# Running only the expert blocks that hold tokens: 24 fixed blocks and an eight-way dispatch

## The chip, the cores and the metric

The kernel runs on one core of one Trainium2 chip. The metric is the device time in microseconds of one execution, and lower is better. Before the change the median of three runs is 627.48 us, the fastest 621.67 us and the slowest 633.91 us.

## The reference

A gated linear attention is followed by a mixture of eight experts. Attention has batch 4, 8 heads, 768 tokens and 48 columns a head:

```python
for t in range(S):
    state = alpha[:, :, t, :, None] * state + np.einsum('bhd,bhe->bhde', k[:, :, t], v[:, :, t])
    y[:, :, t] = np.einsum('bhd,bhde->bhe', q[:, :, t], state)
```

Its output, as 3072 tokens of 384 columns, is `x`. The cosine router gives each token the expert whose embedding is nearest to it, and a gate weight. Each expert then handles its own tokens alone, with `w1[e]` of 384 x 1024 and `w2[e]` of 1024 x 384:

```python
for e in range(E):
    mask = expert_idx == e
    if not mask.any():
        continue
    h = np.maximum(x[mask] @ w1[e], 0.0)
    out[mask] = gate_w[mask, None] * (h @ w2[e])
```

All values are 32-bit floats. How many tokens an expert gets depends on the inputs, which are made from a fixed seed.

## The kernel before

The work has three stages. The first is attention (L99 to L339): 24 chunks of 128 tokens, all heads of a chunk at a time, with the steps of four chunks overlapped. It leaves the rows of `x` in DRAM (`x_rows`) and each token's expert and gate on the chip.

The second is the routing (L342 to L423). Tokens are sorted by expert into blocks of 128 rows, and every expert begins a new block. `nb` is the number of blocks of each expert and `start` the block at which an expert begins. A product of one-hot matrices (`inv`, L398) turns the sort around into `gidx`, the token that each row of each block reads, and `sidx`, the token that it is written to. A row without a token reads token 0 and is written nowhere. `eblk` holds the expert of each block, and `fresh` says whether the block's weights differ from those in its buffer.

The third stage is the experts (L426 to L502). 3072 tokens fill at least 24 blocks, and eight experts with a part-filled last block each can make them 31 (`NBLK`). The kernel runs all 31 in one unrolled loop (L439), however many hold tokens. A block j has these steps, each on its own engine:

- SP reads two numbers into registers (L441, L447) and issues the loads of `w1` and `w2` (L451, L454), 1.5 MB each, into buffer j % 2. From block 2 on, the loads are conditional on `fresh`.
- POOL gathers 128 rows of `x_rows` into `xg` (L459).
- PE turns `xg` in three transposes into `pxg` (L469), and DVE copies it to `xgT` (L471).
- PE multiplies by `w1` into `ph` (L478, 48 matmul instructions), and ACT applies the relu into `hT` (L484).
- PE multiplies by `w2` into `pyo` (L488, 16 instructions), DVE scales by the gate into `y` (L492), and POOL scatters `y` to the output rows (L493).

The scheduler orders the instructions of each engine ahead of time, within straight code. Each engine runs its own list in order and waits by semaphores only. `xg` and `xgT` have three buffers each, so POOL gathers several blocks ahead of PE, and the transposes of two blocks usually stand together ahead of a `ph`. At the end (L528) every engine drains, and SP waits for the last scatters.

Of the kernel before, what the change touches and what calls it, by code (L numbers as in the profile page):

```python
# [9 lines left out]
FP32 = mybir.dt.float32  # L10
I32 = mybir.dt.int32
AF = mybir.ActivationFunctionType
ALU = mybir.AluOpType
# [10 lines left out]
def kernel(  # L24
# [12 lines left out]
    nc = tc.nc  # L37
# [1 line left out]
    E, DM = expert_emb.shape  # L39
    F = w1.shape[2]  # L40
    P = 128
    DP = 64  # a head's columns, padded so that two heads fill the partitions
    NP = H // 2  # pairs of heads
    NCH = S // P  # chunks of a sequence
    N = B * S
    NS = N // P  # slots: token = slot * P + partition
    KT = DM // P
    FT = F // P
    # every expert's tokens fill whole blocks of P rows but for its last one
    NBLK = (N + E * (P - 1)) // P  # L50
    FAR = 1 << 20  # a row index out of bounds: the row is skipped

    x_rows = nc.dram_tensor("x_rows", (N, DM), FP32, kind="Internal").ap()

    consts = ctx.enter_context(tc.tile_pool(name="consts", bufs=1))

# [1 line left out]
    ident = consts.tile([P, P], FP32)  # L58
    make_identity(nc, ident)
    causal = consts.tile([P, 1, P], FP32)  # [j, i] = 1 where j <= i  # L60
    make_upper_triangular(nc, causal[:, 0], val=1.0, diag=True)
    earlier = consts.tile([P, P], FP32)  # [j, i] = 1 where j < i
    make_upper_triangular(nc, earlier, val=1.0, diag=False)
    ones = consts.tile([P, P], FP32)
    nc.gpsimd.memset(ones, 1.0)
    zeros = consts.tile([P, P], FP32)
    nc.gpsimd.memset(zeros, 0.0)
    half = consts.tile([P, NP, 2], FP32)  # which head of the pair a partition is of
    nc.gpsimd.memset(half, 0.0)
    nc.gpsimd.memset(half[0:DP, :, 0:1], 1.0)  # L70
    nc.gpsimd.memset(half[DP:P, :, 1:2], 1.0)
# [3 lines left out]
    nc.vector.tensor_copy(cols, cols_i)  # L75
    toks_i = consts.tile([P, NS], I32)
    nc.gpsimd.iota(toks_i, pattern=[[P, NS]], base=1, channel_multiplier=1)
    toks = consts.tile([P, NS], FP32)  # token + 1
    nc.vector.tensor_copy(toks, toks_i)
    first = consts.tile([P, E], FP32)  # E, E-1, ..: the first of equal logits wins  # L80
    nc.vector.tensor_scalar(first, cols[:, 0:E], -1.0, float(E), ALU.mult, ALU.add)

# [1 line left out]
    lg = consts.tile([P, NS, E], FP32)  # L84
    sq = consts.tile([P, NS], FP32)
    gate = consts.tile([P, NS], FP32)
# [7 lines left out]
    bgate = consts.tile([P, NBLK], FP32)  # L94
    eblk = consts.tile([1, NBLK], I32)
    fresh = consts.tile([1, NBLK], I32)

    # ==== gated linear attention, a chunk of P tokens of all heads at a time ====
    with ExitStack() as c1:  # L99
        pads = c1.enter_context(tc.tile_pool(name="pads", bufs=1))  # L100
        loads = c1.enter_context(tc.tile_pool(name="loads", bufs=6))
# [84 lines left out]
            nc.sync.dma_start(out=vt, in_=v_r[b, c])  # L186

        def decays(s):
            """q and k, head columns on the partitions, with the decays of the chunk.

            a: products of alpha from the chunk's start; r: of those after a token.
            The decay from token j to token i is a[i] / a[end] * r[j].
            """
            c = s % NCH
            d = st[s]
            i = s % NBUF
            pa = turned(at_s[i], "pa")
            a = work.tile([P, NP, P], FP32, name="a")
            r = r_s[s % NR]
            for p in range(NP):  # L200
                nc.vector.tensor_tensor_scan(a[:, p], pa[:, p], zeros, 1.0, ALU.mult, ALU.add)  # L201
                nc.vector.tensor_tensor_scan(  # L202
                    r[:, p, P - 2 :: -1], pa[:, p, P - 1 : 0 : -1], zeros[:, 0 : P - 1],
                    1.0, ALU.mult, ALU.add,
                )
            end = a[:, :, P - 1 : P]
            rend = work.tile([P, NP, 1], FP32, name="rend")
            nc.vector.reciprocal(rend, end)
            if c > 0:
                d["ends"] = ends = work.tile([P, NP, 2], FP32, name="ends", bufs=3)  # L210
                nc.gpsimd.tensor_tensor(ends, half, end.to_broadcast([P, NP, 2]), ALU.mult)
            pk = turned(kt_s[i], "pk")
            d["kr"] = kr = work.tile([P, NP, P], FP32, name="kr", bufs=3)
            nc.vector.tensor_tensor(kr, pk, r, ALU.mult)  # L214
            pq = turned(qt_s[i], "pq")
            d["qs"] = qs = work.tile([P, NP, P], FP32, name="qs", bufs=4)
            for p in range(NP):
                nc.vector.scalar_tensor_tensor(  # L218
                    out=qs[:, p], in0=pq[:, p], scalar=rend[:, p], in1=a[:, p],
                    op0=ALU.mult, op1=ALU.mult,  # L220
                )

        def update(s):
            """The state at the chunk's end, and its decayed form that the queries meet."""
            c = s % NCH
            d = st[s]
            vt, kr = d["vt"], d["kr"]
            decayed = None
            if c > 0:
                d["decayed"] = decayed = work.tile([P, NP, 2, D], FP32, name="decayed", bufs=3)  # L230
                nc.gpsimd.tensor_tensor(  # L231
                    decayed, carried["state"], bc(d["ends"], [P, NP, 2, D], 3), ALU.mult
                )
            if c == NCH - 1:
                return
            pkb = ps_tr.tile([P, NP, P], FP32, tag="tr", name="pkb")
            for p in range(NP):
                nc.tensor.transpose(pkb[:, p], kr[:, p], ident)  # L238
            kb = work.tile([P, NP, P], FP32, name="kb")
            nc.scalar.copy(kb, pkb)  # L240
            pd = ps_mm.tile([P, 512], FP32, tag="mm", name="pd")
            for p in range(NP):
                nc.tensor.matmul(  # L243
                    pd[:, 2 * p * D : 2 * (p + 1) * D],
                    lhsT=kb[:, p],
                    rhs=vt[:, 2 * p : 2 * p + 2].rearrange("p h d -> p (h d)"),
                    start=True, stop=True,
                )
            carried["state"] = state = work.tile([P, NP, 2, D], FP32, name="state")
            sflat = state.rearrange("p n j e -> p (n j e)")  # L250
            if decayed is None:
                nc.scalar.copy(sflat, pd[:, 0:DM])
            else:
                nc.vector.tensor_tensor(  # L254
                    sflat, pd[:, 0:DM], decayed.rearrange("p n j e -> p (n j e)"), ALU.add
                )

        def scores(s):
            """scores[j, i] of every head, zero where j > i."""
            d = st[s]  # L260
            kr, qs = d["kr"], d["qs"]
            d["sm"] = sm = work.tile([P, 2, NP, P], FP32, name="sm")
            sc = ps_sc.tile([P, 2, NP, P], FP32, name="sc")
            for p in range(NP):
                for hh in range(2):
                    sl = slice(DP * hh, DP * hh + DP)
                    nc.tensor.matmul(  # L267
                        sc[:, hh, p], lhsT=kr[sl, p], rhs=qs[sl, p], start=True, stop=True
                    )
            for hh in range(2):  # L270
                nc.vector.tensor_tensor(  # L271
                    sm[:, hh], sc[:, hh], causal.to_broadcast([P, NP, P]), ALU.mult
                )

        def rows(s):
            """The chunk's rows of x: kept in DRAM for the gathers; their squares."""
            d = st[s]
            vt, qs, sm, decayed = d["vt"], d["qs"], d["sm"], d.get("decayed")
            py = ps_mm.tile([P, 512], FP32, tag="mm", name="py")
# [41 lines left out]
            if s % NCH == NCH - 1:  # L321
                choose(s // NCH)

        # each step is a chunk behind the one before it, so that none waits for the last
        load(0)
        load(1)
        prepare_experts()
# [10 lines left out]
            if 0 <= s - 3 < NS:  # L338
                logits(s - 3)  # L339

    # ==== routing: tokens sorted by expert into blocks of P rows ====
    with ExitStack() as c2:  # L342
        rt = c2.enter_context(tc.tile_pool(name="rt", bufs=1))
        ps_rt = c2.enter_context(tc.tile_pool(name="ps_rt", bufs=1, space=PSUM))

        # rank of a token among its expert's tokens, and the experts' totals
        rk = ps_rt.tile([P, (NS + 1) * E], FP32, name="rk")
        nc.tensor.matmul(
            rk, lhsT=ones, rhs=before.rearrange("p s e -> p (s e)"), start=True, stop=False
# [2 lines left out]
            rk[:, 0 : NS * E], lhsT=earlier, rhs=chosen.rearrange("p s e -> p (s e)"),  # L352
            start=False, stop=True,
        )
        # blocks per expert and the block at which each starts
        nb_i = rt.tile([P, E], I32, name="nb_i")
        nb = rt.tile([P, E], FP32, name="nb")
        start = rt.tile([P, E], FP32, name="start")
# [6 lines left out]
        nc.vector.tensor_tensor(start, start, nb, ALU.subtract)  # L365
        nc.vector.tensor_scalar(row0, start, float(P), None, ALU.mult)

        # a token's sorted row, as block and row of the block
        shp = [P, NS, E]
        place = rt.tile(shp, FP32, name="place")  # L370
        nc.vector.tensor_tensor(
# [12 lines left out]
        blk = rt.tile([P, NS], FP32, name="blk")  # L384
        nc.vector.tensor_copy(blk, dest_i)

        # inverse of the sort: [row, block] = token + 1 and gate, zero where there is none
        shp = [P, NS, NBLK]
        in_blk = rt.tile(shp, FP32, name="in_blk")
        nc.vector.tensor_tensor(in_blk, bc(cols[:, 0:NBLK], shp, 1), bc(blk, shp, 2), ALU.is_equal)  # L390
# [13 lines left out]
        tok = rt.tile([P, NBLK], FP32, name="tok")  # L404
        nc.vector.tensor_scalar(tok, inv[:, 0], -1.0, None, ALU.add)
        nc.vector.tensor_copy(bgate, inv[:, 1])
        # a row without a token reads token 0 and is written nowhere
        nc.vector.tensor_scalar(gidx, tok, 0.0, None, ALU.max)
        none = rt.tile([P, NBLK], FP32, name="none")
        nc.vector.tensor_scalar(none, tok, 0.0, float(FAR), ALU.is_lt, ALU.mult)  # L410
        nc.vector.tensor_tensor(sidx, tok, none, ALU.add)

        # a block's expert, and whether its weights are not yet in the block's buffer
        shp = [1, NBLK, E]
        past = rt.tile(shp, FP32, name="past")
        nc.vector.tensor_tensor(
# [5 lines left out]
        nc.vector.memset(fresh[:, 0:2], 1)  # L422
        nc.vector.tensor_tensor(fresh[:, 2:], of[:, 2:], of[:, 0 : NBLK - 2], ALU.not_equal)  # L423

    # ==== the experts, a block of P sorted tokens at a time ====
    with ExitStack() as c3:  # L426
        wpool = c3.enter_context(tc.tile_pool(name="wpool", bufs=1))
        xp = c3.enter_context(tc.tile_pool(name="xp", bufs=3))
# [7 lines left out]
        w1_r = w1.rearrange("e (k p) f -> e p k f", p=P)  # L436
        w2_r = w2.rearrange("e (k p) d -> e p k d", p=P)

        for j in range(NBLK):  # L439
            w1_t, w2_t = w1_s[j % 2], w2_s[j % 2]  # L440
            e = nc.values_load(  # L441
                eblk[0:1, j : j + 1], engines=(SP,), min_val=0, max_val=E - 1,
# [58 lines left out]
            tc.declare_no_dep(ins.ins, group="rows", reason="blocks hold different tokens")  # L501
            tc.add_to_no_dep_group("rows", ins.ins)  # L502


# [1 line left out]
_INS = ['q', 'k', 'v', 'alpha', 'moe_expert_emb', 'moe_tau', 'moe_w1', 'moe_w2']  # L506
# [26 lines left out]
```

## Time and profile before

| | |
|---|---|
| median of three runs (lowest, highest) | 627.48 us (621.67, 633.91) |
| span of the profiled execution | 625.4 us |
| profiled execution's own time | not listed apart from its span |
| PE busy (matmul) | 554.2 us, 89% |
| DVE, ACT, POOL busy | 201.9, 100.9 and 93.7 us |
| attention and routing | 0 to about 254 us |
| experts, 31 blocks | about 254 us to the end |

The span is the time from the first to the last instruction of one execution. PE is TensorE's matmuls, PEld its weight loads, DVE VectorE, ACT ScalarE, POOL GpSimd and SP SyncE. A q behind an engine's name (POOLq, SPq) marks its sequencer or its queue. Rows of a timeline give the start, the duration, the engine, the line, the operation and, in brackets, the idle time before it and what ended that. A merged row (x48) is many instructions of one kind. Lines are those of the kernel above.

### The profile page before, as it was taken

The numbers are of one execution on the slowest core, as the hardware profiler recorded it, in microseconds if no ns is written. First come the engines' busy times: TensorE is split into PE (matmuls) and PEld (weight loads), VectorE is DVE, ScalarE is ACT, GpSimd is POOL, SyncE is SP. The second block draws the span as 40 slices with busy tenths as digits, with TensorE's granted clock in tenths as the row PEclk, the third lists the DMA queues.
The fourth block names the chain that finished last, engine by engine and source line by source line (L and its number), as shares of the span: only waits on it lengthen the run. The fifth ranks groups of instructions, "written<-read, shape, count | busy, mean of one in ns | idle before, by whom it ended". The sixth has DMA issues, their size and how long they took to land.

```text
span 625.4 us, 9640 instructions
## 1 busy us (share of the span) xinstructions
PE 554.2 (89%) x3804; PEld 463.9 (74%) x3804; DVE 201.9 (32%) x608; ACT 100.9 (16%) x202; POOL 93.7 (15%) x149
## 2 busy tenths in 40 slices
PE   5799989889989965389999999999999999999994
PEld 4688878788878855268778787787877877878773
DVE  6967676757765527101010010100101001010010
ACT  2222422422241240001101011011110100101100
POOL 1110110010011101311011120220211112011010
PEclk9999999988995985579999999999999999999998
DMA  9979886636710000760757658166175775811000
GB/s 152 173 128 150 126 123 124 129 67 124 129 39 14 26 25 2 260 243 26 249 181 244 236 192 275 38 239 219 51 248 195 233 258 166 298 39 38 0 1 0
DMA packets 130508, 85.37 MB, mean 137 GB/s; under 512 B 102199, under 2 KB 121699, under 8 KB 130464
## 3 DMA queue, kind: packets, MB, share of 16 engines
q1 hardware_dynamic: 126336, 73.93, 46.4%
q0 software_dynamic: 3968, 10.82, 4.9%
q8 instruction: 30, 0.49, 0.3%
q14 instruction: 14, 0.11, 0.1%
q10 hardware_dynamic: 160, 0.01, 0.0%
HBM read 122.50 MB, written 10.81 MB: 213 GB/s over the span
## 4 chain that ended last, share of the span: by engine, by line
PE 72%; DVE 13%; issue 8%; ACT 2%; DMA 2%; POOL 1%; POOLq 0%; ACTq 0%
PE ph L478 24%; PE pyo L488 22%; PE py L292 7%; PE py L283 4%; DVE a L201 4%; PE pd L243 3%; DVE r L202 3%; PE pl L316 3%; DMA xg<-x_rows,gidx 2%; PE pa L174 2%; PE inv L398 2%; PE sc L267 2%; DVE kr L214 1%; PE px L309 1%; DVE xgT L471 1%
## 5 line engine op out<-in xcount | busy, mean ns | idle before, releaser
L478 PEld LDWEIGHTS ph<-xgT,w 128*128 128x128 f32 x1488 | 172.1, 194 | 14.3 <-DVE xgT L471 9.8
L478 PE MATMUL ph<-xgT,w 128*128 128x128 f32 x1488 | 174.6, 278 | 6.8 <-DVE xgT L471 6.8
L488 PE MATMUL pyo<-w,hT 128*128 128x384 f32 x496 | 165.1, 486 | 0.0
L488 PEld LDWEIGHTS pyo<-w,hT 128*128 128x128 f32 x496 | 91.9, 190 | 57.5
L492 DVE TENSOR_SCALAR y<-pyo,bgate 128x384 f32<-128x384 f32 x31 | 19.2, 618 | 303.1 <-PE pyo L488 303.1
L484 ACT ACTIVATE hT<-ph 128x512 f32<-128x512 f32 x62 | 37.0, 597 | 345.2 <-PE ph L478 345.2
L493 POOL DMA_INDIRECT out_dram<-y,sidx x31 | 31.1, 1003 | 178.8 <-DVE y L492 175.2
L292 PE MATMUL py<-vt,sm 128*128 128x48 f32 x384 | 56.4, 277 | 0.0
L292 PEld LDWEIGHTS py<-vt,sm 128*128 128x128 f32 x384 | 53.0, 203 | 0.0
L459 POOL DMA_INDIRECT xg<-x_rows,gidx x31 | 32.2, 1037 | 135.4 <-PE pxg L469 115.0
L201 DVE TENSOR_TENSOR_SCAN a<-pa,zeros 128x128 f32<-128x128 f32 x96 | 38.9, 405 | 22.0 <-PE pa L174 22.0
L202 DVE TENSOR_TENSOR_SCAN r<-pa,zeros 128x127 f32<-128x127 f32 x96 | 38.1, 397 | 0.0
L283 PE MATMUL py<-decayed,qs 128*128 128x96 f32 x160 | 35.6, 306 | 0.0
L271 DVE TENSOR_TENSOR sm<-sc,causal 128x512 f32<-128x512 f32 x48 | 31.1, 679 | 1.9 <-PE sc L267 1.9
L267 PE MATMUL sc<-qs,kr 64*128 64x128 f32 x384 | 30.6, 302 | 0.0
L267 PEld LDWEIGHTS sc<-qs,kr 64*128 64x128 f32 x384 | 25.6, 203 | 4.7 <-issue 3.8
L243 PE MATMUL pd<-vt,kb 128*128 128x96 f32 x160 | 23.3, 290 | 4.7 <-ACT kb L240 4.7
L231 POOL TENSOR_TENSOR decayed<-state,ends 128x384 f32<-128x384 f32 x20 | 16.6, 830 | 71.1 <-DVE state L254 56.9
L238 PE MATMUL pkb<-ident,kr 128*128 128x128 f32 x80 | 13.4, 291 | 15.5 <-DVE r L202 15.5
L469 PE MATMUL pxg<-ident,xg 128*128 128x128 f32 x93 | 15.0, 298 | 13.7 <-issue 8.5
L218 DVE SCALAR_TENSOR_TENSOR qs<-pq,rend,a 128x128 f32<-128x128 f32 x96 | 27.0, 341 | 0.0
L243 PEld LDWEIGHTS pd<-vt,kb 128*128 128x128 f32 x160 | 20.0, 196 | 8.9 <-ACT kb L240 8.9
(115 smaller groups left out, 382.4 us busy)
## 6 DMA issues: line engine op xcount, KB each, us to landing
w<-in_moe_w_dram SPq DMA_DIRECT2D x62, 1536.0 KB
at<-in_alpha_dram SPq DMA_DIRECT2D x24, 192.0 KB
qt<-in_q_dram SPq DMA_DIRECT2D x24, 192.0 KB
kt<-in_k_dram SPq DMA_DIRECT2D x24, 192.0 KB
vt<-in_v_dram SPq DMA_DIRECT2D x24, 192.0 KB
x_rows<-x SPq DMA_DIRECT2D x24, 192.0 KB
xg<-x_rows,gidx POOLq DMA_INDIRECT x31, 5.4
out_dram<-y,sidx POOLq DMA_INDIRECT x31, 3.0
```

The source lines that it names most:

```text
L201: nc.vector.tensor_tensor_scan(a[:, p], pa[:, p], zeros, 1.0, ALU.mult, ALU.add)
L202: nc.vector.tensor_tensor_scan(r[:, p, P - 2 :: -1], pa[:, p, P - 1 : 0 : -1], zeros[:, 0 : P - 1], 1.0, ALU.mult, ALU.add,)
L243: nc.tensor.matmul(pd[:, 2 * p * D : 2 * (p + 1) * D], lhsT=kb[:, p], rhs=vt[:, 2 * p : 2 * p + 2].rearrange("p h d -> p (h d)"), start=Tr ...
L267: nc.tensor.matmul(sc[:, hh, p], lhsT=kr[sl, p], rhs=qs[sl, p], start=True, stop=True)
L271: nc.vector.tensor_tensor(sm[:, hh], sc[:, hh], causal.to_broadcast([P, NP, P]), ALU.mult)
L283: nc.tensor.matmul(py[:, 2 * p * D : 2 * (p + 1) * D], lhsT=qs[:, p], rhs=decayed[:, p].rearrange("p j e -> p (j e)"), start=not opened, s ...
L292: nc.tensor.matmul(py[:, h * D : (h + 1) * D], lhsT=sm[:, hh, p], rhs=vt[:, h], start=not opened, stop=True, skip_group_check=True,)
L459: nc.gpsimd.indirect_dma_start(out=xg, out_offset=None, in_=x_rows, in_offset=bass.IndirectOffsetOnAxis(ap=gidx[:, j : j + 1], axis=0), bo ...
L478: nc.tensor.matmul(ph[:, f], lhsT=w1_t[:, i, (f0 + f) * P : (f0 + f + 1) * P], rhs=xgT[:, i], start=(i == 0), stop=(i == KT - 1),)
L484: nc.scalar.activation(hT[:, f0 : f0 + 4], ph, AF.Relu)
L488: nc.tensor.matmul(py, lhsT=hT[:, f], rhs=w2_t[:, f], start=(f == 0), stop=(f == FT - 1))
L493: ins = nc.gpsimd.indirect_dma_start(out=out, out_offset=bass.IndirectOffsetOnAxis(ap=sidx[:, j : j + 1], axis=0), in_=y, in_offset=None, ...
```

## The change

The loop body becomes a function `block(j)`, unchanged inside. Blocks 0 to 23 always run. A new number `nmore` is the count of blocks in use less 24. It is read into a register of every engine behind block 23, and an eight-way jump takes each engine into one of eight arms. Arm n holds blocks 24 to 23 + n as straight code of its own, so arm 0 is empty and arm 7 has seven blocks. Two small DVE instructions compute `nmore` in the routing. The rest of the diff takes comments out.

```diff
+    nmore = consts.tile([1, 1], I32)
...
+        nc.vector.tensor_tensor(
+            nmore, start[0:1, E - 1 : E], nb[0:1, E - 1 : E], ALU.add
+        )
+        nc.vector.tensor_scalar(nmore, nmore, -NS, None, ALU.add)
...
-        for j in range(NBLK):
+        def block(j):
             w1_t, w2_t = w1_s[j % 2], w2_s[j % 2]
...
+        for j in range(NS):
+            block(j)
+        more = nc.values_load(
+            nmore, min_val=0, max_val=NBLK - NS,
+            skip_runtime_bounds_check_because="N rows fill NS to NBLK blocks",
+        )
+        for n in tc.Switch(more, NBLK - NS + 1):
+            for j in range(NS, NS + n):
+                block(j)
```

## Rows read from the trace of the kernel before

**Rows 1.** The page: busy time and instructions; busy tenths and GB/s in 40 slices.
```profile
PE 554.2 (89%) x3804; PEld 463.9 (74%) x3804; DVE 201.9 (32%) x608; ACT 100.9 (16%) x202; POOL 93.7 (15%) x149
...
PE   5799989889989965389999999999999999999994
...
GB/s 152 173 128 150 126 123 124 129 67 124 129 39 14 26 25 2 260 243 26 249 181 244 236 192 275 38 239 219 51 248 195 233 258 166 298 39 38 0 1 0
```
**Rows 2.** Chain of waits in order of time: start, us, engine, group; blocks 0, 23, 24, 25.
```profile
270.60 7.42 PE ph L478 x48
...
528.78 5.62 PE ph L478 x48
534.41 5.16 PE pyo L488 x16
539.57 5.36 PE ph L478 x48
...
551.27 5.62 PE ph L478 x48
```
**Rows 3.** Busy time by stretch over the last blocks (last three columns: granted clock, DMA share, GB/s).
```profile
562.00:578.00 16.00, 15.48 (x109) 13.07 (x108) 2.16 (x4) 1.79 (x3) 3.05 (x3) 1.00 0.11 37
578.00:594.00 16.00, 16.00 (x91) 12.16 (x90) 0.62 (x1) 1.79 (x3) 1.00 (x1) 1.00 0.00 0
```
**Rows 4.** Timeline of the end: PE's last `pyo`, then `y` and its scatter.
```profile
614.79 2.74 PE L488 MATMUL pyo<-w,hT 128*128 128x384 f32 x8
...
617.57 0.62 DVE L492 TENSOR_SCALAR y<-pyo,bgate 128x384 f32<-128x384 f32 x1 [9.90 <-PE pyo L488]
618.47 0.98 POOL L493 DMA_INDIRECT out_dram<-y,sidx  x1 [9.54 <-DVE y L492]
```
**Rows 5.** Timeline where the expert stage begins: first weights, first gather, transposes, copy.
```profile
253.58 0.41 SPq L451 DMA_DIRECT2D w<-in_moe_w_dram  x1
253.99 1.21 POOL L459 DMA_INDIRECT xg<-x_rows,gidx  x1 [11.97 <-DVE sidx L411]
...
261.11 2.65 PE L469 MATMUL pxg<-ident,xg 128*128 128x128 f32 x9 [8.54 <-issue]
...
262.07 0.56 DVE L471 COPY xgT<-pxg 128x384 f32<-128x384 f32 x1 [8.75 <-PE pxg L469]
```
**Rows 6.** Gathers into `xg` over 250 to 330 us, and all scatters of L493: landing.
```profile
DMA to landing us min/median/max: 3.1/6.0/6.8
...
DMA to landing us min/median/max: 2.1/3.0/7.9
```
**Rows 7.** Line L441 on SP's queue, durations in ns; and the page's instruction queue.
```profile
L441 SPq TENSOR_LOAD <-eblk x31: 263/272/467, 237.3 to 584.7; - x31
...
q8 instruction: 30, 0.49, 0.3%
```
**Rows 8.** Stretches of PE alone; last columns granted clock, DMA share, GB/s.
```profile
272.00:274.00 2.00, 2.00 (x11) 0.50 1.06 373
...
276.00:280.00 4.00, 4.00 (x26) 1.00 0.00 0
```
**Rows 9.** Timeline of SP: second load of block 23, both of block 24, first of 26.
```profile
517.12 0.08 SPq L454 DMA_DIRECT2D w<-in_moe_w_dram  x1
522.48 0.38 SPq L451 DMA_DIRECT2D w<-in_moe_w_dram  x1
527.64 0.38 SPq L454 DMA_DIRECT2D w<-in_moe_w_dram  x1
...
544.96 0.09 SPq L451 DMA_DIRECT2D w<-in_moe_w_dram  x1
```
**Rows 10.** Line L528, a closing semaphore of PE: durations in ns, first and last start.
```profile
L528 PEldq EVENT_SEMAPHORE  x2: 51/51/51, 624.8 to 625.4; - x2
```
**Rows 11.** Timeline of the routing: DVE at `row0`, and `past` behind it.
```profile
235.82 0.17 DVE L366 TENSOR_SCALAR row<-start 128x8 f32<-128x8 f32 x1
235.90 0.40 DVE L416 TENSOR_TENSOR past<-cols,start 1x248 f32<-1x248 f32 x1
```

## The prediction

> **What bounds the kernel now.** I first read the slices of the page [rows 1]. From slice 18 on PE is at nine tenths or more until the last slice, so the expert stage is bound by PE, and whatever is taken from PE's list there comes off the end. Next I followed the chain of waits through that stage [rows 2]. It alternates `ph` and `pyo` of one block after another, with almost nothing but PE on it. A block is 10.52 us of matmuls (5.36 + 5.16) when no transposes stand in between. Counting its `ph` groups from the first at 270.60, the one at 528.78 is block 23, and its `pyo` ends at 539.57. Blocks 24 to 30 follow.
>
> How many of those hold tokens shows in what the DMAs move. In 562 to 578 us there are two scatters (blocks 25 and 26) and one gather, and 37 GB/s over 16 us is 592 KB, three times 128 rows of 1536 bytes. In 578 to 594 us PE computes all the time and the scatter of block 27 moves 0 GB/s [rows 3]. The last three slices of the page read 0, 1 and 0 [rows 1]. Blocks 27 to 30 therefore write nothing: 27 blocks are in use, `nmore` is 3, and the changed kernel should run 27 blocks instead of 31.
>
> **What is removed.** From the end of block 23 (539.57) to PE's last `pyo` (614.79 + 2.74 = 617.53 [rows 4]) the seven blocks take 77.96 us. Only three remain, and the stretch is rebuilt below.
>
> **The three blocks kept.** All three gathers can be issued together (`xg` and `xgT` have three buffers), so their transposes fall into the wait at the front, and the blocks run back to back: 3 x 10.52 = 31.56 us at full clock.
>
> **What is added: one break in the pipeline.** Now POOL gathers several blocks ahead. Behind the change the gather of block 24 lies in an arm, and POOL reaches it only when its whole list of blocks 0 to 23 is done. The last item there is the scatter of block 23, which needs `y` of block 23, which needs PE's last matmul of that block. So PE runs dry at 539.57 and waits for this chain:
>
> - `y` and the scatter. Before, the last `pyo` ends at 617.53 and the scatter's issue at 618.47 + 0.98 = 619.45 [rows 4]: 1.92 us.
> - The dispatch on POOL. Reading the number costs 0.27 us on SP [rows 7], the nearest row for POOL. No row shows a jump. What it may have to wait for is its code: the instruction queue moved 30 pieces of 16 KB in 0.3% of 16 engines' span [rows 7], which is 0.003 x 16 x 625.4 / 30 = 1.0 us each, and the shortest landing of any scatter after its issue is 2.1 us [rows 6]. Lower bound 0.3 us (code already there). Upper bound 8 us, the longest landing of a scatter being 7.9. I take 0.3 + 0.3 for address and jump + 2.1 = 2.7 us, because the code is one piece and 2.1 is the nearest row for a small isolated transfer.
> - The gather: 3.1 to 6.8 us from issue to landing at the beginning of the expert stage [rows 6], where weights load as well. Those of block 25 will also be loading, so I take the median, 6.0.
> - Landing to first matmul. The first gather was issued at 253.99 and landed 6.8 us later, at 260.8; the transposes started at 261.11, and the copy ended at 262.07 + 0.56 = 262.63 [rows 5]. With 0.2 us to the matmul this is 2.0 us.
>
> Together 1.92 + 2.7 + 6.0 + 2.0 = 12.6 us in which PE has no work (bounds 1.92 + 0.3 + 3.1 + 2.0 = 7.3 and 1.92 + 8 + 6.8 + 2.0 = 18.7).
>
> On the chip's code the Trainium skill speaks against this change ("Runtime: NRT & Kernel Launch", section "Instruction fetch mechanics"): a taken branch whose target lies outside the fetched window stalls until the page arrives, one reason it gives for full unrolling. By that rule the 2.1 us are due on every engine; without it the break would be 10.5 us and the gain 2.1 us larger. No row of this kernel shows a jump.
>
> The other engines take the same jump behind longer covers. DVE's and PE's lie beside POOL's dispatch and gather, about 9 us; ACT is done before block 23's `pyo`. If that cover were gone, PE's own dispatch, 2.7 us by the same sum, would be due. SP is moved past its own dispatch too. It has issued block 23's second load at 517.12 and next needs to act at 522.48, when block 24's first load may start [rows 9]: 5.3 us of slack. Both loads of block 24 are real (0.38 us of issue against 0.08 for a skipped one), and block 26 reuses block 24's buffer. They are issued from 522.48 and 527.64, 17 and 12 us before PE has finished block 23, so they stay hidden while SP's dispatch takes under 5.3 us.
>
> **The clock.** Before the first experts PE had stood idle for 8.5 us ahead of the transposes [rows 5]. It started `ph` at 270.60 [rows 2], its granted clock was still 0.50 in 272 to 274, and 1.00 from 276 on [rows 8]. 0.50 is 1.2 GHz, 1.00 is 2.4 GHz. That first `ph` took 7.42 us against 5.36 at full clock [rows 2]: 2.1 us. The break is as long as that idle stretch or longer, so I charge 2.1 us once (bounds 0 and 2.1).
>
> **The end.** Before, 7.9 us lie between the last matmul, 617.53 [rows 4], and the end of the span. The last scatter there moves nothing; now it moves 128 rows. Each engine also jumps out of its arm and brings its semaphores level. Lower bound 0; upper 6 us, a scatter's 2.1 to 7.9 [rows 6]. I take 2.5, about one isolated transfer and a few semaphore steps of 0.05 [rows 10].
>
> **The two small instructions** cost 0.17 us each like their neighbours [rows 11]. `past` starts 0.08 us behind the previous instruction there, in the pause of a dependent chain, so part is free: 0.2 us (0 to 0.4).
>
> **The sum.** -77.96 + 31.56 + 12.6 + 2.1 + 2.5 + 0.2 = -29.0 us. Against the span of 625.4 us that is 596.4. The median of the runs is 627.48, 2.1 us above that span, so the forecast is 598.5 us, 4.6% faster. With all low bounds the change is -77.96 + 31.56 + 7.3 = -39.1 (588.4 us); with all high bounds -77.96 + 31.56 + 18.7 + 2.1 + 6 + 0.4 = -19.2 (608.3 us).
>
> **Rivals.**
>
> *The engines meet at the dispatch.* If SP too is held until block 23 has ended, loads and gathers of blocks 24 and 25 start together, as at 253.58. There the first `ph` came 17.0 us behind the first load's issue (270.60 less 253.58 [rows 2, 5]). The break becomes 1.92 + 2.7 + 17.0 = 21.6 instead of 12.6, and the time 607.5 us. For it: each engine reads the same number. Against it: every wait in this profile is a semaphore between two instructions, and nothing in the change makes SP wait for PE beyond its own buffers. Chance 0.10.
>
> *Leaving costs a count.* If the unequal arms are brought level by one semaphore step for each instruction left out, PE pays for 4 blocks of 134 (64 matmuls, 64 weight loads, 6 for the transposes), 536 x 0.051 us [rows 10] = 27 us at the end: 625.8 us, no change. Against it: a semaphore can take a larger step at once. Chance 0.05.
>
> *The code in between is streamed, not jumped over.* At the entry lie arms 0 to 2 with 3 blocks, at the exit arms 4 to 7 with 22, together 25 x 134 instructions on PE; 30 pieces served its 7608 instructions [rows 1, 7], so 256 fit one and this is 13 pieces, some 19 with each arm on its own boundary. At 1.0 us each the gain shrinks to 10 us (617.5, no change). At 3.0 us each, the median landing of a small scatter [rows 6], 57 us are added and the kernel is slower, 655 us. It is slower by over 2% when a piece costs more than (29.0 + 12.5) / 19 = 2.2 us. Before, fetches lie hidden under long PE work; nothing shows what an exposed one costs. Against it: a jump names its target. Chance 0.06, of which 0.04 slower.
>
> *It doesn't drop the blocks.* With seven blocks run behind the break, 7 x 10.52 replaces the 31.56 and the time is 640.6 us, slower. The bytes say three [rows 3]. Chance 0.01.
>
> **How the numbers follow.** The forecast has 0.78. The median and the extremes before differ by about 6 us, so a measurement tells about 2% from no change, 615 to 640 us. Forecast and meeting together give 0.88 of faster; for the spread of the runs I take 0.87. No change has 0.08 (leaving 0.05, streaming 0.02, spread 0.01), slower 0.05 (streaming 0.04, all blocks 0.01). The range takes the bounds of the forecast, with the meeting inside them, and some of the runs' spread: 588 to 612.
>
> **What would show it.** In the trace after: 27 gathers and 27 scatters, 1296 `ph` matmuls; a hole in PE of about 12.6 us behind block 23, ended by the transposes of block 24 with its gather as releaser; a read of `nmore` on each engine; a gap on POOL of about 2.7 us between block 23's scatter and block 24's gather; block 24's loads issued before block 23 ends; a first `ph` of about 7.6 us in the arm, then 5.4. I am wrong if the hole is over 25 us, if PE waits for `w` in the arm, if the end grows past 14 us, or if blocks 0 to 23 no longer run at two per 22.5 us (551.27 less 528.78 [rows 2]).

## The result and the profile after

The changed kernel takes 603.27 us (median of four runs, 600.23 to 605.2), against 624.62 us for the kernel before on the same chip (median of four runs as well). The ratio is 0.964, 95% interval 0.957 to 0.971: faster by 3.6%. The ratios and intervals, here and below, leave out runs that fell to a lower granted clock, so they need not equal the quotient of the medians. The forecast for the median was 598.5 us. The profiled execution took 600.23 us, with a span of 598.5 us; the forecast for the span was 596.4 us.

The page has 27 blocks where it had 31, and one short valley in PE near the end:

```profile
PE 512.8 (86%) x3536; PEld 430.7 (72%) x3536; DVE 197.9 (33%) x602; ACT 96.1 (16%) x194; POOL 85.1 (14%) x141
...
PE   5799889979988993729999999999999999991993
...
L484 PE MATMUL ph<-xgT,w 128*128 128x128 f32 x1296 | 153.4, 279 | 5.5 <-DVE xgT L477 5.5
```

1296 `ph` matmuls are 27 x 48. The slice with a 1 stands where [rows 1] had nines throughout. The timeline there, from the end of block 23 on:

```profile
534.38 5.33 PE L494 MATMUL pyo<-w,hT 128*128 128x384 f32 x16
...
539.74 0.37 SPq L460 DMA_DIRECT2D w<-in_moe_w_dram  x1
539.75 0.62 DVE L498 TENSOR_SCALAR y<-pyo,bgate 128x384 f32<-128x384 f32 x1 [10.88 <-PE pyo L494]
540.64 0.98 POOL L499 DMA_INDIRECT out_dram<-y,sidx  x1 [10.98 <-DVE y L498]
548.91 1.05 POOL L465 DMA_INDIRECT xg<-x_rows,gidx  x1 [7.28 <-DMA xg<-x_rows,gidx]
...
551.57 1.00 POOL L465 DMA_INDIRECT xg<-x_rows,gidx  x1 [0.30 <-issue]
...
552.16 0.88 PE L475 MATMUL pxg<-ident,xg 128*128 128x128 f32 x3 [12.45 <-DMA xg<-x_rows,gidx]
...
555.36 6.83 PE L484 MATMUL ph<-xgT,w 128*128 128x128 f32 x48
```

Block 23 ends at 539.71. The `ph` of block 24 starts at 555.36: 15.65 us without a matmul of an expert, where [rows 2] had no gap. POOL scatters block 23 at 540.64 and issues the gather of block 24 only at 548.91. That row names an earlier gather as what ended the wait, but block 23's had landed by 527.6, when it was transposed. What POOL does in between stands in the chain of waits, which lists its sequencer (POOLq):

```profile
540.41 0.51 POOLq L512
...
541.11 0.05 POOLq L544
...
541.19 0.04 POOLq L544
541.23 5.94 issue
547.17 0.06 POOLq L516
...
547.30 0.73 another core or an unknown queue
```

It reads the number (L512, 0.51 us), works out the address and jumps at 541.19. The next row is the first instruction of the arm, at 547.17. "Issue" is time in which the engine waited for nothing that the profile shows: 5.94 us. Behind it stands another 0.73 us for a semaphore step of the software DMA queue that each of the six gathers and scatters of this arm has ahead of it (INC_SWDGE_SEM).

The other engines take the same jump. The rows of L512 are the reads, those of L544 the jumps, those of L516 the first instruction of the arm; the two times with "to" are the first and the last start:

```profile
L512 SPq TENSOR_LOAD <-nmore x1: 273/273/273, 517.4 to 517.4; - x1
...
L516 SPq BRANCH_PREFETCH_HINT  x1: 56/56/56, 520.4 to 520.4; - x1
L516 ACTq BRANCH_PREFETCH_HINT  x1: 52/52/52, 541.2 to 541.2; - x1
L516 PEldq BRANCH_PREFETCH_HINT  x1: 50/50/50, 542.6 to 542.6; - x1
L516 DVEq BRANCH_PREFETCH_HINT  x1: 56/56/56, 546.8 to 546.8; - x1
...
L544 SPq COMPARE_BRANCH  x2: 43/50/58, 517.9 to 567.7; - x2
L544 ACTq COMPARE_BRANCH  x2: 48/50/53, 535.3 to 583.3; - x2
L544 PEldq COMPARE_BRANCH  x2: 322/3358/6394, 536.1 to 583.9; - x2
L544 DVEq COMPARE_BRANCH  x2: 60/64/69, 540.6 to 588.4; - x2
```

ACT needs 535.3 to 541.2, PE 536.1 to 542.6 (6.39 of it on the jump itself), DVE 540.6 to 546.8: about 6 us each. SP needs only 517.9 to 520.4, 2.5 us. The DMA engines were busy for 0.83 to 0.90 of the time in the long waits, and for 0.22 in SP's. That difference is the thread for the experiments.

### The profile page after: what moved, and what is told of

It reads as the page before. It is cut to its first block, busy times and chain, and to the rows that moved or that the text cites. A ratio compares the mean times of both kernels' runs of the same rounds, so it can differ in the third digit from the quotient of the medians.

```text
span 598.5 us, 9056 instructions
## 1 busy us (share of the span) xinstructions
PE 512.8 (86%) x3536; PEld 430.7 (72%) x3536; DVE 197.9 (33%) x602; ACT 96.1 (16%) x194; POOL 85.1 (14%) x141
## 4 chain that ended last, share of the span: by engine, by line
PE 70%; DVE 13%; issue 9%; ACT 3%; DMA 2%; another core or an unknown queue 1%; POOL 1%; POOLq 0%; ACTq 0%
PE ph L484 22%; PE pyo L494 21%; PE py L293 7%; PE py L284 4%; DVE a L202 4%; PE pd L244 4%; DVE r L203 4%; PE pl L317 3%; DMA xg<-x_rows,gidx 2%; PE pa L175 2%; PE inv L399 2%; PE sc L268 2%; DVE kr L215 2%; PE px L310 1%
## 5 line engine op out<-in xcount | busy, mean ns | idle before, releaser
L484 PEld LDWEIGHTS ph<-xgT,w 128*128 128x128 f32 x1296 | 151.4, 196 | 11.9 <-DVE xgT L477 7.9
L484 PE MATMUL ph<-xgT,w 128*128 128x128 f32 x1296 | 153.4, 279 | 5.5 <-DVE xgT L477 5.5
L494 PE MATMUL pyo<-w,hT 128*128 128x384 f32 x432 | 143.8, 486 | 0.0
L494 PEld LDWEIGHTS pyo<-w,hT 128*128 128x128 f32 x432 | 80.0, 190 | 50.1
L498 DVE TENSOR_SCALAR y<-pyo,bgate 128x384 f32<-128x384 f32 x27 | 16.7, 618 | 263.7 <-PE pyo L494 263.7
L490 ACT ACTIVATE hT<-ph 128x512 f32<-128x512 f32 x54 | 32.2, 597 | 320.9 <-PE ph L484 320.9
L499 POOL DMA_INDIRECT out_dram<-y,sidx x27 | 27.0, 1001 | 187.6 <-DVE y L498 185.2
L465 POOL DMA_INDIRECT xg<-x_rows,gidx x27 | 27.9, 1032 | 105.8 <-PE pxg L475 77.9
L475 PEld LDWEIGHTS pxg<-ident,xg 128*128 128x128 f32 x81 | 10.9, 162 | 33.3 <-issue 30.4
L477 DVE COPY xgT<-pxg 128x384 f32<-128x384 f32 x27 | 14.1, 550 | 42.0 <-PE pxg L475 23.5
L219 DVE SCALAR_TENSOR_TENSOR qs<-pq,rend,a 128x128 f32<-128x128 f32 x96 | 26.9, 340 | 0.0
```

Source lines behind the costliest of these rows:

```text
L465: nc.gpsimd.indirect_dma_start(out=xg, out_offset=None, in_=x_rows, in_offset=bass.IndirectOffsetOnAxis(ap=gidx[:, j : j + 1], axis=0), bo ...
L484: nc.tensor.matmul(ph[:, f], lhsT=w1_t[:, i, (f0 + f) * P : (f0 + f + 1) * P], rhs=xgT[:, i], start=(i == 0), stop=(i == KT - 1),)
L490: nc.scalar.activation(hT[:, f0 : f0 + 4], ph, AF.Relu)
L494: nc.tensor.matmul(py, lhsT=hT[:, f], rhs=w2_t[:, f], start=(f == 0), stop=(f == FT - 1))
L499: ins = nc.gpsimd.indirect_dma_start(out=out, out_offset=bass.IndirectOffsetOnAxis(ap=sidx[:, j : j + 1], axis=0), in_=y, in_offset=None, ...
```

## The experiments

The profiles differ in when block 0 starts. In the nine of this study its first `ph` lies between 265.3 and 278.3 us, while blocks 0 to 23 take 268.0 to 269.4 us in all of them. The difference is the clock granted in the attention stage, ahead of anything the change touches: over the first 225 us it is 0.97 in the two profiles that reach block 0 first, 0.95 before and after the change, and 0.89 in the one that reaches it last. Two of the experiments, each up to just before its block 0 (last three columns: granted clock, DMA share, GB/s):

```profile
0.00:265.00 265.00, 208.11 (x1741) 187.40 (x1742) 169.25 (x549) 63.94 (x140) 36.80 (x94) 0.90 0.59 112
```
```profile
0.00:278.00 278.00, 222.65 (x1741) 201.76 (x1742) 169.78 (x551) 64.19 (x140) 37.03 (x94) 0.84 0.54 107
```

The first has 27 blocks in straight code, the second the count forced to seven. They run the same attention, at 0.90 and 0.84 of the clock. So the table compares within each profile. The expert stage runs from block 0's first `ph` to the end of the span, the hole from block 23's last `pyo` to block 24's first `ph`, and the end from the last `pyo` to the end of the span. A dispatch ahead of block 0 can also cost something before the first `ph`, which the expert stage leaves out. So one column more begins earlier, at `sidx`, the last step of the routing ahead of the first gather.

Each median and ratio is taken against the kernel before in the same set of runs. For the first four (straight code to dispatch ahead of block 0) the comparison with it counts as unclear, although each interval lies below 0.97; what is concluded rests on the stages.

| kernel | blocks run | expert stage, us | hole, us | end, us | `sidx` to the end of the span, us |
|---|---|---|---|---|---|
| before | 31 | 355.0 | 0 | 7.9 | 372.3 |
| changed | 27 | 327.8 | 15.7 | 10.1 | 345.3 |
| 27 blocks in straight code | 27 | 309.5 | 0 | 7.4 | 326.9 |
| prefetch hint | 27 | 323.8 | 11.1 | 10.2 | 341.3 |
| gathers ahead of the dispatch | 27 | 321.9 | 8.4 | 10.7 | 339.9 |
| dispatch ahead of block 0 | 27 | 308.3 | 0 | 7.2 | 327.1 |
| no weight loads in block 25 | 27 | 324.8 | 12.7 | 10.1 | 342.4 |
| count forced to seven | 31 | 372.6 | 18.9 | 7.9 | 389.9 |
| the same, dispatch ahead of block 0 | 31 | 353.9 | 0 | 7.9 | 372.7 |

**27 blocks in straight code.**

```diff
...
-        for j in range(NS):
-            block(j)
-        more = nc.values_load(nmore, ...)
-        for n in tc.Switch(more, NBLK - NS + 1):
-            for j in range(NS, NS + n):
-                block(j)
+        for j in range(27):
+            block(j)
```

> 27 blocks in straight code, no count of blocks and no jump (it leaves the four empty blocks out for these inputs alone). It prices the dispatch as a whole. Theory A (the hole behind block 23 and the end are all that the dispatch costs): block 27 began at 573.75 us in the trace of before, so the span is 573 to 574 us plus an end of 8 to 10 us, 581 to 584 us, 15 to 17 us under the changed kernel's 598.5, with two blocks per 22.5 us throughout. Rival (the split also slows blocks 0 to 23 or the three blocks of the arm): the span is under 578 us, and the difference to the changed kernel shows outside the hole.

The median is 582.74 us against 628.14 before (ratio 0.937, 0.925 to 0.948). The expert stage is 309.5 us, 18.3 less than with the dispatch. The hole (15.65) and the end (10.07 - 7.41 = 2.66) give all of it. The last three blocks take 33.0 us in the one and 33.2 in the other: the slow first `ph` of the arm costs what the transposes between the blocks cost in straight code. The span of 574.8 is under the expected 581 to 584, and under the rival's 578, because block 0 began 5 us early; blocks 0 to 23 take 269.1 us, as before, and the difference to the changed kernel lies in the hole and the end. Theory A stands: the dispatch costs what the hole and the end cost. The four empty blocks alone were worth 355.0 - 309.5 = 45.5 us.

**A prefetch hint ahead of the jump.**

```diff
-        for j in range(NS):
-            block(j)
         more = nc.values_load(nmore, ...)
-        for n in tc.Switch(more, NBLK - NS + 1):
+        ET = mybir.EngineType
+        every = {e: more for e in (ET.PE, ET.DVE, ET.Activation, ET.Pool, ET.SP)}
+        for j in range(NS):
+            if j == NS - 1:
+                tc.switch_hint(every, NBLK - NS + 1, "tail")
+            block(j)
+        for n in tc.Switch(more, NBLK - NS + 1, hint="tail"):
...
```

> The changed kernel with the count read ahead of block 23 and a prefetch hint for the jump put there on all five engines. Theory A (each engine's 5.9 to 6.4 us behind its jump is a wait for the code of the arm): the wait falls to under 1 us on POOL, the hole from 15.6 to about 9.5 us, the span to about 592 us. Rival B (POOL's 5.9 us is the scatter of block 23 finishing, or a fixed price of the jump): the wait stays at 5.9 us and the span at 598 us.

POOL's sequencer in the chain of waits, from the jump on:

```profile
537.55 0.06 POOLq L548
537.61 0.47 POOL out_dram L499
...
538.11 0.04 POOLq L465
```

The first gather of the arm (L465) is at hand 0.5 us behind the jump, where 5.94 us had passed. The scatter of block 23 is the same one, so it was not what POOL waited for; rival B falls, and the 5.94 us were the wait for code. ACT and SP too are in the arm 0.5 us behind their jumps, and PE's jump takes 1.03 us. DVE alone still waits 4.4 us, until 541.4; why is not shown, and it is off the path here, since the gather lands later. The hole is 11.1 us, not 9.5: the gather now started at 539.74, while the loads of block 25 were running, and its transposes only at 545.24, 5.5 us later against 3.25 in the changed kernel (busy share of the DMA engines 0.97 in 540 to 545 us here, 0.20 in 547 to 552 us there). The median is 593.35 us (ratio 0.949, 0.939 to 0.959).

**The gathers ahead of the dispatch.**

```diff
...
+            xg = late.get(j)
+            if xg is None:
+                xg = xp.tile([P, DM], FP32, name="xg")
+                gather(j, xg)
...
         for j in range(NS):
             block(j)
+            if j == NS - 4:
+                for i in range(NS, NBLK):
+                    late[i] = wpool.tile([P, DM], FP32, name=f"xl{i}")
+                    gather(i, late[i])
```

> The gathers of blocks 24 to 30 are issued ahead of the dispatch, into buffers of their own (seven gathers, always); the transposes and all else stay in the arms. Theory A (POOL's way through the dispatch to the gather and its landing sets the hole; every other engine also waits 6 us for its code): the hole is ended by DVE, whose jump comes behind y of block 23: 0.6 + 6.2 + 0.6 for the copy + 0.2 = about 7.8 us in place of 15.6, span about 590 us. Rival B (only POOL is held, by its scatter): PE goes on once its own transposes and copy are done, a hole of about 3 us, span about 586 us. Rival C (seven gathers bunched on POOL delay the scatters and hold PE earlier): blocks 20 to 23 run slower than 22.5 us a pair and the gain is under 3 us.

The timeline of its hole, behind block 23's end at 541.86:

```profile
544.56 0.86 PE L482 MATMUL pxg<-ident,xl 128*128 128x128 f32 x6 [2.70 <-issue]
548.90 1.02 DVE L484 COPY xgT<-pxg 128x384 f32<-128x384 f32 x2 [6.39 <-issue]
...
550.21 7.24 PE L491 MATMUL ph<-xgT,w 128*128 128x128 f32 x48
```

PE has its code at 544.5 and transposes two blocks at once. The copy waits until 548.90 with "issue" as the reason: DVE jumped at 542.8 and had its code at 548.7. The hole is 8.4 us (7.8 expected), theory A; for rival B PE would have gone on at about 545. With POOL out of the way DVE is late next. The span is 594.4 us, not about 590: block 0 began 1.8 us later than in the changed kernel, and the slow first `ph` and the end took about 1 us more. Blocks 0 to 23 took 269.4 us as ever, so rival C falls too. The median is 596.12 us (0.948, 0.934 to 0.962).

**The dispatch ahead of block 0.**

```diff
         more = nc.values_load(nmore, ...)
         for n in tc.Switch(more, NBLK - NS + 1):
-            for j in range(NS, NS + n):
+            for j in range(NS + n):
                 block(j)
```

> The dispatch is put ahead of block 0: eight arms of 24 to 31 blocks, of which the fourth (27 blocks) runs. Theory A (a jump costs only what it stalls in a pipeline that is full): POOL, PE, ACT and SP take it while they wait for the routing, DVE's 6 us lie under the first gather (6.8 us), no hole behind block 23, span within 3 us of the kernel with 27 blocks in straight code. Rival (code that is run from an arm is fetched late all along, or seven times the code costs something by itself): 5 us and more above it, with PE's pauses spread over the blocks.

First instructions of the arm (L514) and jumps (L542):

```profile
L514 ACTq BRANCH_PREFETCH_HINT  x1: 52/52/52, 240.1 to 240.1; - x1
L514 SPq BRANCH_PREFETCH_HINT  x1: 50/50/50, 240.5 to 240.5; - x1
L514 POOLq BRANCH_PREFETCH_HINT  x1: 60/60/60, 243.3 to 243.3; - x1
L514 PEldq BRANCH_PREFETCH_HINT  x1: 50/50/50, 255.5 to 255.5; - x1
L514 DVEq BRANCH_PREFETCH_HINT  x1: 56/56/56, 259.7 to 259.7; - x1
...
L542 ACTq COMPARE_BRANCH  x2: 48/50/53, 237.4 to 567.9; - x2
L542 SPq COMPARE_BRANCH  x2: 43/50/58, 237.8 to 550.7; - x2
L542 POOLq COMPARE_BRANCH  x2: 43/56/70, 240.6 to 573.7; - x2
...
L542 PEldq COMPARE_BRANCH  x2: 312/1808/3304, 252.2 to 568.6; - x2
...
L542 DVEq COMPARE_BRANCH  x2: 60/64/69, 254.1 to 573.1; - x2
```

ACT, SP and POOL jump while the routing still runs, and have their code 2.7 us later, long before the first gather at 254.05. PE jumps at 252.2 and has its code 3.3 us later, DVE at 254.1 and 5.6 us later, both before that gather has landed. The expert stage is 308.3 us, against 309.5 for straight code. But that leaves out what comes before the first `ph`. From `sidx` on, first straight code, then this kernel:

```profile
247.98 0.19 DVE L411 TENSOR_TENSOR sidx<-tok,none 128x31 int32<-128x31 f32 x1
...
265.33 7.57 PE L477 MATMUL ph<-xgT,w 128*128 128x128 f32 x48
```
```profile
253.20 0.19 DVE L412 TENSOR_TENSOR sidx<-tok,none 128x31 int32<-128x31 f32 x1
...
271.96 6.54 PE L484 MATMUL ph<-xgT,w 128*128 128x128 f32 x48
```

The first `ph` starts 18.76 us behind `sidx` in place of 17.35, 1.4 us later, and is itself 1.0 us shorter. From `sidx` to the end it is 327.1 us against 326.9: the dispatch costs some 0.2 us here, not nothing. The median is 584.54 us (ratio 0.936, 0.929 to 0.943). Its interval lies wholly under that of the changed kernel (0.957 to 0.971), although the two were timed in different sets of runs. Theory A stands, and of the versions that choose at run time this is the one to keep. It was run with 27 blocks and, below, with 31.

**Block 25 without its weight loads.** So far the waits were short where the DMA engines had little to move (2.5 to 2.8 us, on PE 3.3, at a busy share of 0.03 to 0.22) and long while weights loaded (5.6 to 6.4 us at 0.81 to 0.90). This run leaves out the loads of block 25, which then multiplies by the weights that lie in its buffer.

```diff
+            if j != NS + 1:
                 nc.sync.dma_start(out=w1_t, ..., cond=cond)
                 nc.sync.dma_start(out=w2_t, ..., cond=cond)
```

> The changed kernel without the two weight loads of block 25 (it leaves them out, and block 25 multiplies by the weights that lie in its buffer). These are the loads that run while PE, ACT, DVE and POOL wait for the arm's code. Theory A (the code comes through the same DMA engines as the weights, and shares them): POOL's and DVE's wait behind the jump falls from 5.9 and 6.1 us to the 2.5 to 2.8 us that SP had here and ACT, SP and POOL had where the dispatch stood ahead of the experts; the hole goes from 15.6 to about 12.3 us, the time from block 0's first ph to the end of the span from 327.8 to about 324.5. Rival B (the wait belongs to the engine or to the length of its code): it stays at 5.9 us and the hole at 15.6.

POOL's sequencer again:

```profile
542.54 0.04 POOLq L545
542.57 2.97 issue
545.55 0.06 POOLq L517
```

2.97 us in place of 5.94. DVE's wait fell from 6.1 to 3.0 us (542.0 to 545.1), ACT's from 5.8 to 2.7, PE's from 6.4 to 3.6, the hole to 12.7. So the code arrives beside the weights, and while they load it takes about twice as long. Rival B falls. The median of two runs, 601.71 us, tells little from the changed kernel's 603.27; the stage tells more, 324.8 against 327.8 us.

**The count forced to seven**, where the dispatch stands behind block 23:

```diff
-        nc.vector.tensor_scalar(nmore, nmore, -NS, None, ALU.add)
+        nc.vector.tensor_scalar(nmore, nmore, 0, NBLK - NS, ALU.mult, ALU.add)
```

> The changed kernel with the count forced to seven, so that all 31 blocks run behind the dispatch: what it costs on inputs that fill every block. Theory A (the price is the hole, the slow first ph and the end, whatever the arm): 598.5 + 4 x 11.24 = 643 us of span, 1.03 times the kernel before. Rival B (a longer arm adds waits of its own for code on PE, ACT or POOL): over 648 us, with further holes in PE beyond block 24.

The median is 646.83 us against 626.97 before, ratio 1.034 (1.026 to 1.041): inputs that fill all 31 blocks pay 3.4%. The stage is 372.6 us, 17.6 over the kernel before, near theory A's sum. The profiled span, 650.9 us, is over the expected 643 and over rival B's 648, but block 0 began 7.6 us later than in the changed kernel. Not foreseen: the hole is 18.9 us. In this arm the scheduler put the transposes of five blocks ahead of the first `ph`, and the last two wait for their gathers:

```profile
562.75 0.87 PE L475 MATMUL pxg<-ident,xg 128*128 128x128 f32 x3 [1.49 <-DMA xg<-x_rows,gidx]
...
564.59 0.87 PE L475 MATMUL pxg<-ident,xg 128*128 128x128 f32 x3 [0.96 <-DMA xg<-x_rows,gidx]
...
565.25 8.01 PE L484 MATMUL ph<-xgT,w 128*128 128x128 f32 x48
```

Rival B falls: from block 24's first `ph` to the last `pyo` PE has no pause over 0.6 us in this arm of seven.

**The count forced to seven, the dispatch ahead of block 0** (both edits above).

> The dispatch ahead of block 0, with the count forced to seven: all 31 blocks in one arm. Theory A (ahead of block 0 the dispatch lies under the routing): from block 0's first ph to the end 353 to 356 us as in the kernel before (354.8), a ratio to it of 1.00. Rival B (part of the dispatch is paid): 3 us or more above.

The expert stage is 353.9 us, against 355.0 in the kernel before, as theory A has it. From `sidx` on it is 372.7 against 372.3: some 0.5 us is paid, far from rival B's 3. The median of 630.53 us beside 626.97 has no ratio on record; the stage within the profile settles it.

## Why the prediction was right

The direction, the mechanism and the sum held, and each step can be read off. That the sum came so near is in part luck, since the terms of the break err both ways and the end came out right for another reason than forecast. In span the change was forecast at -29.0 us and came to 625.4 - 598.5 = -26.9.

- **Blocks dropped.** `nmore` was 3 and 27 blocks ran, read from the bytes of the scatters [rows 3]. Three blocks and their slow first `ph` take 588.39 - 555.36 = 33.0 us; forecast 31.56 + 2.1.
- **The break**, 12.6 us forecast, is 15.65, inside its bounds of 7.3 to 18.7. The chain was right, and three of its four links were mis-sized. `y` and the scatter: 1.92 forecast, 541.62 - 539.71 = 1.91 measured. Dispatch: 2.7 forecast, 548.91 - 541.62 = 7.29 measured. Landing of the gather: 6.0 forecast, 552.16 - 548.91 = 3.25 measured, because by then the loads of block 25 were done. Landing to the first `ph`: 2.0 forecast, 3.20 measured, since the transposes of all three blocks stand ahead of the first `ph`, and the third waited for its own gather.
- **Where the dispatch term failed** is the nearest row chosen for code. I took the shortest landing of a scatter, 2.1 us [rows 6], as the price of one isolated piece. That is nearly what an engine pays on quiet DMAs (2.5 to 3.1 us, on PE 3.3 to 3.7). But the jump came while weights were loading [rows 9], and there it is 5.9. The read and the jump cost nothing, as they lay beside the scatter; 5.55 us of the wait stuck out behind it. The last 1.74 us lie between the arm's first instruction and the gather, 0.73 of them the semaphore step, and the forecast had no term for these. The errors of dispatch and landing hang together: the code waited for the weights in the gather's place, and the gather then found the DMAs free. The hint shows the exchange: with the code at hand the gather met the loads.
- **The rule against jumps** ("Runtime: NRT & Kernel Launch", section "Instruction fetch mechanics", of the Trainium skill) is borne out: the first instruction of the arm came 5.94 us behind POOL's jump, and within 0.5 us with the hint.
- **The two small instructions** took 0.14 and 0.13 us. From the first matmul of the routing to `sidx` it is 20.4 us in place of 20.3; forecast 0.2 us more.
- **The clock.** While PE had no matmul the granted clock fell from 1.00 in 543 to 544 us to 0.50 (1.2 GHz) in 545 to 546. It was still 0.50 when the first `ph` began, and 0.98 in 558 to 560. That first `ph` in the arm took 6.83 us against 5.52, 1.3 us; forecast 2.1.
- **The end** grew by 2.2 us; forecast 2.5, and that these agree is luck. The forecast charged the bytes of the last scatter and the semaphore steps. In straight code the same scatter is there and the end is 7.4 us, under the 7.9 of before, so its bytes add nothing that shows. The 2.66 us over straight code are about what POOL spends from the jump out of the arm, at 590.4, to its first drain at 593.0:

```profile
L544 POOLq DRAIN  x3: 45/112/4567, 593.0 to 598.2; - x3
...
L544 POOLq COMPARE_BRANCH  x2: 38/54/70, 541.2 to 590.4; - x2
```

  The same step takes 0.5 us with the count forced to seven, and with the dispatch ahead of block 0, and there the end is 7.2 to 7.9 us. Why it is short there is not shown.

- **SP's slack** held: SP read the number at 517.4, had its code at 520.4 and issued block 24's loads before block 23 had ended:

```profile
522.62 0.40 SPq L457 DMA_DIRECT2D w<-in_moe_w_dram  x1
527.78 0.38 SPq L460 DMA_DIRECT2D w<-in_moe_w_dram  x1
```

  So the engines do not meet at the dispatch. PE and DVE had their code at 542.6 and 546.8, under POOL's 547.2, as forecast.
- **The other rivals.** One semaphore step for each instruction left out would have shown as 27 us at the end; 2.2 are there. Streaming the code in between would have shown as some 13 to 19 pieces more on the instruction queue of [rows 7]. It moved 31, against 28 for the same blocks in straight code; the smaller queue, of half as large pieces, moved 28 against 13, over five engines and two jumps each. With the dispatch ahead of block 0 the unused arms hold 193 blocks, and the two queues moved 31 and 26. All seven blocks did not run; forced to, they gave 646.83 us where 640.6 was named.
- **Run to run.** The forecast counted on about 6 us of spread without saying where it comes from. Between the nine profiles it lies in the attention stage, in the granted clock.

## What to carry to other kernels

A run-time jump in the middle of a full pipeline costs little for the jump itself (0.04 to 0.06 us on SP, ACT, DVE and POOL). It costs the wait for the arm's code, and what every engine was doing ahead of time: no engine reaches into the arm before its own list in front of it is done, so prefetches stop there. Put it where the engines wait anyway, here under the routing, even if the arms together then hold seven times the code (220 blocks for 31): 18.3 us became 0.2 to 0.5. When you move a cost to another place, measure from a point ahead of both places. If the jump must stand in the middle, move the loads that the arm needs first ahead of it (5.9 us less in the expert stage here), hint the jump (4.0 us), and keep bulk loads out of that moment (3.0 us). The three were run one at a time; what they give together is not shown.

## What the hardware showed that was not expected

- The wait for an arm's code is 2.5 to 3.1 us (3.3 to 3.7 on PE) where the DMA engines are busy for 0.03 to 0.33 of the time, and 5.4 to 6.4 us while 1.5 MB loads run (0.81 to 0.90); leaving out two such loads turned 5.94 into 2.97 on POOL.
- Reading one number into a register took 0.47 to 0.55 us on ACT, PE, POOL and DVE, and on SP 0.27 us in the middle of the experts but 0.47 us ahead of them; the row of SP [rows 7] was too low a price for POOL.
- In the changed kernel's arm of three blocks each of the six software DMAs had a semaphore step of about 0.72 us ahead of it (INC_SWDGE_SEM). In the arm of 27 there were eight such steps of 0.13 us, and in the arms of seven and of 31 none. What decides this is not shown.
- The wait behind a jump is not booked where one would look: on PE it is the length of the jump (6.39 us), on the other engines it is idle time that the chain calls "issue".
